# Two batches at a time in the body of a linear-attention and squared-ReLU kernel, ungated weight loads, and an order table in place of a planner

## The chip, the cores and the metric

One core of a Trainium2 chip runs the whole program. Its engines are TensorE (PE in the profile; PEld is its weight loads), VectorE (DVE), ScalarE (ACT), GpSimd (POOL) and SyncE (SP), beside 16 DMA engines that SP, ACT and POOL feed through queues of their own. The metric is device time in microseconds, from launch to end. A profiled execution also has a span: from the first to the last instruction that the profile shows.

## The reference

Four batches, eight heads, 768 steps, 48 channels per head. For each batch and head a 48 x 48 state is carried over the steps; its output goes, 384 channels wide, into a two-layer network with a squared ReLU.

```python
for t in range(S):
    kt, vt, rt = k[:, :, t], v[:, :, t], r[:, :, t]
    cur = einsum('bhd,bhe->bhde', u[None] * kt, vt)
    y[:, :, t] = einsum('bhd,bhde->bhe', rt, state + cur)
    state = w[None, :, :, None] * state + einsum('bhd,bhe->bhde', kt, vt)
x = y.transpose(0, 2, 1, 3).reshape(B * S, H * D)      # 3072 x 384
g = np.maximum(x @ w_in, 0.0) ** 2                      # w_in: 384 x 2048
return g @ w_out                                        # w_out: 2048 x 384
```

All inputs and the output are float32; the kernel multiplies in bfloat16.

## The kernel before

**Units.** The 768 steps are cut into 6 chunks of 128, so there are 24 units (chunk, batch), numbered 4 * chunk + batch. Within a chunk the recurrence becomes matrix products. Each unit goes through these steps, which the planner's keys and the order table name:

- `rt`, `kt`, `vt`: loads of r, k, v. For units 0 to 5 r and k come as two half loads with a row order of their own; later units load the 192-byte rows of all heads in one DMA. r and k are issued by SP, v by POOL, there behind a small copy (`gate`) that waits until k of the unit before has landed.
- `scale` (DVE, twice): r and k times powers of the decay, into `rkw` (bfloat16, heads padded to 64).
- `rkT`: r and k turned to channel-major. Units 0 to 5 by PE transposes (`turn`) and ACT copies, with `kb`, `kbT` turning k back; later units by one transposing DMA on SP (L476).
- `rk` (DVE), `at` (PE, L521: 8 products of 64 rows, k times q), `mask` (DVE, twice), `s` (PE: row sums `d` for the current step's term, and the state product), `dv`, `sadd`, `sdec` (DVE), `stb` (ACT), `y` (PE, L576 and, from chunk 1, L582), `yb` (DVE).
- `xT`: the unit's output turned, by PE and ACT (`xturn`) for units 0 to 5, later by a transposing DMA on SP (L600).
- `m1` (PE, L623): input product, 4 steps of 12 matmuls of 128 x 128 columns, each with its own 128 columns of `w_in_q` as stationary operand; `relu` (ACT), `sq` (ACT or DVE).
- `m2` (PE, L647): output product, 4 steps of 4 matmuls with 384 columns; `osb` (ACT) and `out` (SP store). The last unit does m2 in two halves (L663).

**Weights.** `w_in_q` and `w_out_q` are four tiles each, cast on the way by POOL's DMAs: `I.0` to `I.3` and `O.0` to `O.3`. Each waits behind a `gate` copy until some r or k has landed (`FRONT`, L277; L442).

**Order.** Nothing is scheduled at run time: each engine runs its instructions in the order in which the program emits them. Before, `Plan.run` (L47) makes this order on the host from costs, ranks and due times; `GROUPS` and `PAIRED` (L281, L282) leave every unit by itself. While PE has nothing to do in the first 16 planned microseconds, it runs `fill` matmuls (L380) on a constant tile. `bank` gives each product one of eight PSUM banks.

Of the kernel before, what the change touches and what calls it, by code (L numbers as in the profile page):

```python
# [16 lines left out]
class Plan:  # L17

    def __init__(self, lags, cold, spare, turns):
        self.turns = turns
        self.lags = lags
        self.cold = cold  # L30
        self.spare = spare
        self.steps = []
        self.at = {}
        self.users = {}
        self.place = {}

    def add(self, key, engine, cost, emit, needs=(), rank=0.0, new=(), uses=(), move=None):
        kind, which = (key[0], key[1] if len(key) == 2 else key[1:]) if isinstance(key, tuple) else ("", key)
        rank = self.turns.get(kind, {}).get(which, rank)
        s = dict(key=key, engine=engine, cost=cost, emit=emit, rank=rank, new=new, move=move)  # L40
        s["needs"] = [n for n in needs if n is not None]
        self.at[key] = s
        self.steps.append(s)
        for x in tuple(new) + tuple(uses):
            self.users.setdefault(x, []).append(s)

    def run(self, room, banks, count):  # L47
        todo = {}
        for s in self.steps:
            todo.setdefault(s["engine"], []).append(s)  # L50
        for mine in todo.values():
            mine.sort(key=lambda s: s["rank"])
        rings = {name: [] for name in room}
        free = {e: 0.0 for e in todo}
        queues = {e: [] for e in todo}
        held = {n: None for n in range(count)}
        since = {n: 0.0 for n in range(count)}
        begin, until, tight, loose = self.spare
        free["SP"] = 0.74
        held[0] = "fill"  # L60
        order = []
        t = 0.0
        left = len(self.steps)
        tiny = 1e-9

        moved, chained, left_pe, to_pe, near = self.lags

        def ready(s, e):
            if s["move"]:
                return s["end"] + moved + s["move"][4]  # L70
            if s["engine"] == "PE":
                return s["end"] + (chained if e == "PE" else left_pe)
            return s["end"] + (to_pe if e == "PE" else near)

        marks = []

        def mark(s):
            for e in ("PE", ""):
                heappush(marks, ready(s, e))

        def done(s, e):
            return "end" in s and ready(s, e) <= t + tiny

        def fits(s):
            e = s["engine"]
            names = [x[0] for x in s["new"]]
            for name in set(names):
                if name in banks:
                    continue
                ring, m = rings[name], room[name]  # L90
                for n in range(len(ring) - m, len(ring) - m + names.count(name)):
                    if n >= 0 and not all(done(x, e) for x in self.users[ring[n]]):
                        return False
            wanted = [name for name in names if name in banks]
            if wanted:
                for n, x in held.items():
                    if x not in (None, "fill") and all(done(u, e) for u in self.users[x]):
                        held[n], since[n] = None, max(u["end"] for u in self.users[x])
                if sum(x is None for x in held.values()) < len(wanted):
                    return False  # L100
                for name in set(wanted):
                    mine = sum(x is not None and x[0] == name for x in held.values())
                    if mine + wanted.count(name) > banks[name]:
                        return False
            return True

        while left:
            if held[0] == "fill" and t > until:
                held[0] = None
            for e, mine in todo.items():  # L110
                if free[e] > t + tiny:
                    continue
                if e == "PE" and t < begin - tiny:
                    free[e] = begin
                    continue
                for s in mine:
                    if s["move"] and sum(x[1] / x[0]["move"][0] * x[0]["move"][3] for x in queues[e]) > 1.5:
                        continue
                    if all(done(self.at[k], e) for k in s["needs"]) and fits(s):
                        mine.remove(s)  # L120
                        left -= 1
                        for x in s["new"]:
                            if x[0] in banks:
                                n = 4 + x[1] if x[0] == "log" else min((n for n in held if held[n] is None), key=lambda n: since[n])
                                held[n] = x
                                self.place[x] = n
                            else:
                                rings[x[0]].append(x)
                        s["start"] = t
                        free[e] = t + s["cost"] * (self.cold[1] if e == "PE" and t < self.cold[0] else 1.0)  # L130
                        if s["move"]:
                            queues[e].append([s, s["move"][0], free[e] + s["move"][2]])
                        else:
                            s["end"] = free[e]
                            mark(s)
                        order.append(s)
                        break
                else:
                    if e == "PE" and t < until:
                        free[e] = t + (tight * self.cold[1] if t < self.cold[0] else loose)  # L140
                        order.append(dict(key="fill", emit=self.fill, start=t, end=free[e], engine="PE"))
            heads = [q[0] for q in queues.values() if q]
            moving = [x for x in heads if x[2] <= t + tiny]
            whole = sum(x[0]["move"][1] for x in moving)
            later = [f for f in free.values() if f > t + tiny]
            while marks and marks[0] <= t + tiny:
                heappop(marks)
            later += marks[:1]
            later += [x[2] for x in heads if x[2] > t + tiny]
            later += [t + x[1] * whole / x[0]["move"][1] for x in moving]  # L150
            if not later:
                if left:
                    raise ValueError("nothing can go on: " + str([s["key"] for m in todo.values() for s in m[:3]]))
                break
            step = min(later) - t
            t += step
            for x in moving:
                x[1] -= step * x[0]["move"][1] / whole
                if x[1] <= 1e-7:
                    queues[x[0]["engine"]].pop(0)  # L160
                    x[0]["end"] = t
                    mark(x[0])
        return order
# [3 lines left out]
def kernel(  # L167
# [20 lines left out]
    NQ = 4  # L188
    NPE = 6
    NKE = 6  # L190
    NPY = 6
    NPAD = 8
    NVB = 8
    LATE = (0.2, 0.2, 0.4)
    MOST = 3
    SQUARES = 'AAAMAAAM'
    TURNS = {
        "": {
            "zeros": 38.551
        },  # L200
        "O": {
            0: 76.019, 1: 91.228, 2: 107.535, 3: 7
        },
        "rt": {
            0: -83.003, 1: -66.162, 12: 22.377, 13: 28.231, 14: 28.49, 15: 33.657, 3: -36.29, 5: 1.476, 8: 3.237
        },
        "kt": {
            0: -80.584, 1: -55.486, 10: 19.508, 11: 20.529, 2: -47.443, 6: 2.358
        },
        "at": {  # L210
            0: -3.958, 11: 34.671, 4: -16.745, 7: 10.944
        },
        "mask": {
            (1, 0): -39.238, (10, 0): 33.02, (2, 1): 25.375, (5, 1): 1.515
        },
        "sadd": {
            1: 9.124, 4: 45.244
        },
        "rk": {
            2: 13.012, 7: 14.32, 8: 68.867, 9: -12.042  # L220
        },
        "sums": {
            11: 49.353, 2: -24.778, 8: 5.082
        },
        "dv": {
            2: -26.848, 7: 34.164, 9: -12.993
        },
        "stb": {
            2: -9.741, 4: 57.421
        },  # L230
        "scale": {
# [294 lines left out]
    def at_pair(i):  # L526
        at(i)
        at(i + 1)
# [361 lines left out]
```

## Time and profile before

| | |
|---|---|
| median of 3 runs (lowest to highest) | 175.59 us (175.58 to 175.65) |
| the profiled execution's span | 174.3 us |
| PE, PEld busy | 166.7 us (96%), 134.7 us (77%) |
| ACT, DVE, POOL busy | 132.1, 121.1, 40.0 us |
| DMA packets | 76474, 28.93 MB |
| `fill` matmuls | 98 |

The profiled execution's own time is its span and what lies around it; the median of the runs is 1.3 us above the span. A row of the chain of waits gives start, duration and what was on the chain: an engine and source line with the number of instructions, or a DMA. In a table by stretches of time the columns are busy time of each engine with its number of instructions, the granted TensorE clock, the mean share of the 16 DMA engines and the rate. The page's busy times count overlaps once; "mean ns" is one instruction's own duration, which for pipelined matmuls is longer than their distance.

### The profile page before, as it was taken

To read this page: it belongs to the slowest core of one execution; us is meant where nothing else is said; L and a number is where in the kernel's file an instruction comes from. 1 tells how busy PE (TensorE), PEld (TensorE's weight loads), DVE (VectorE), ACT (ScalarE), POOL (GpSimd) and SP (SyncE) were. 2 spreads that over 40 slices of the span, in tenths; PEclk is the share of its full clock that TensorE was granted. 3 is DMA by queue.
4 is the path that set the end of the run, shared out by engine and by line. 5 is a ranking of instruction groups with operands and counts; after the bars stand their busy time and mean duration, and the time that the engine had idled before them with its cause. 6 is when DMAs were issued, how large, how long until landed. Compare 5 with 4: busy or idle time off the path is not lost.

```text
span 174.3 us, 5795 instructions
## 1 busy us (share of the span) xinstructions
PE 166.7 (96%) x2390; PEld 134.7 (77%) x2390; DVE 121.1 (70%) x252; ACT 132.1 (76%) x268; POOL 40.0 (23%) x84
## 2 busy tenths in 40 slices
PE   7978899999999999999999999999999999999991
PEld 6766799887687787886896787869787698877871
DVE  7869976615999899977986799794989635531010
ACT  3946999999458797886968876939994869948640
POOL 7866890300140220302032202203202000000000
PEclk9999999999999999999999999999999999999999
DMA  4889999999999999999999999999999971130121
GB/s 97 228 179 246 232 218 193 185 221 118 170 201 164 178 154 209 200 214 170 231 142 183 156 237 214 218 177 141 186 200 175 271 180 26 26 111 6 47 81 56
DMA packets 76474, 28.93 MB, mean 166 GB/s; under 512 B 65440, under 2 KB 75296, under 8 KB 76448
## 3 DMA queue, kind: packets, MB, share of 16 engines
q1 hardware_dynamic: 70848, 20.56, 69.8%
q0 software_dynamic: 5312, 7.87, 23.9%
q8 instruction: 18, 0.29, 0.8%
q10 hardware_dynamic: 288, 0.15, 0.4%
q14 instruction: 8, 0.07, 0.1%
HBM read 20.50 MB, written 4.72 MB: 145 GB/s over the span
## 4 chain that ended last, share of the span: by engine, by line
PE 81%; DMA 11%; SPq 4%; issue 1%; DVE 0%; POOL 0%; POOLq 0%
PE bank L623 35%; PE bank L647 33%; DMA w_in_q<-in_moe_w_in_dram 5%; SPq L436 4%; DMA rkT<-rkw 4%; PE bank L521 4%; DMA rt<-in_r_dram 2%; PE bank L576 2%; PE bank L582 2%; PE bank L546 2%; PE bank L663 2%; PE bank L541 1%; PE bank L487 0%; PE bank L607 0%; POOL gate L442 0%
## 5 line engine op out<-in xcount | busy, mean ns | idle before, releaser
L623 PE MATMUL bank<-xT,w_in_q 128*128 128x128 bf16 x1152 | 70.7, 219 | 0.1
L623 PEld LDWEIGHTS <-w_in_q 128*128 128x128 bf16 x1152 | 66.5, 98 | 3.1 <-DMA w_in_q<-in_moe_w_in_dram 0.3
L647 PE MATMUL bank<-w_out_q,g 128*128 128x384 bf16 x368 | 66.9, 326 | 0.0
L631 ACT ACTIVATE gr<-bank 128x512 f32<-128x512 f32 x96 | 54.3, 599 | 13.6 <-PE bank L623 13.3
L647 PEld LDWEIGHTS <-g 128*128 128x128 bf16 x368 | 33.3, 98 | 19.8
L638 ACT ACTIVATE g<-gr 128x512 bf16<-128x512 f32 x72 | 43.7, 637 | 0.4
L533 DVE TENSOR_TENSOR am<-bank,smask 128x512 bf16<-128x512 f32 x48 | 31.3, 682 | 3.3 <-PE bank L521 3.1
L640 DVE TENSOR_TENSOR g<-gr 128x512 bf16<-128x512 f32 x24 | 16.5, 686 | 21.5 <-ACT gr L631 21.5
L465 POOL COPY gate<-kt 128x1 f32<-128x1 f32 x22 | 5.8, 266 | 80.9 <-DMA kt<-in_k_dram 80.9
L654 ACT COPY osb<-bank 128x384 f32<-128x384 f32 x23 | 11.0, 483 | 15.8 <-PE bank L647 15.8
L467 POOL DMA_DIRECT2D vt<-in_v_dram x24 | 21.4, 893 | 5.9 <-issue 1.6
L555 DVE TENSOR_TENSOR dv<-vb,bank 128x384 f32<-128x384 bf16 x24 | 13.2, 548 | 5.3 <-PE bank L546 3.4
L513 DVE TENSOR_TENSOR rk<-rkT 128x512 bf16<-128x512 bf16 x24 | 10.0, 417 | 7.7 <-DMA rkT<-rkw 4.3
L591 DVE TENSOR_TENSOR yb<-bank,dv 128x384 bf16<-128x384 f32 x24 | 13.2, 550 | 2.8 <-PE bank L582 2.4
L471 ACT CAST vb<-vt 128x384 bf16<-128x384 f32 x24 | 12.4, 518 | 0.0
L458 DVE TENSOR_TENSOR rkw<-rt,wpos 128x384 bf16<-128x384 f32 x18 | 9.8, 550 | 1.4 <-DMA rt<-in_r_dram 1.4
L458 DVE TENSOR_TENSOR rkw<-kt,wneg 128x384 bf16<-128x384 f32 x18 | 9.9, 549 | 0.9 <-DMA kt<-in_k_dram 0.9
L567 ACT CAST stb<-st 128x384 bf16<-128x384 f32 x20 | 10.4, 519 | 0.0
L380 PE MATMUL bank<-warm 128*128 128x128 bf16 x98 | 9.3, 248 | 1.1 <-DVE warm L322 1.1
L521 PE MATMUL bank<-rkT 64*128 64x128 bf16 x192 | 9.5, 219 | 0.2
L494 ACT COPY rkT<-bank 128x512 bf16<-128x512 bf16 x12 | 6.8, 588 | 3.0 <-PE bank L487 3.0
L563 DVE TENSOR_TENSOR st<-st,wend 128x384 f32<-128x384 f32 x16 | 8.8, 549 | 0.0
(74 smaller groups left out, 129.1 us busy)
## 6 DMA issues: line engine op xcount, KB each, us to landing
vt<-in_v_dram POOLq DMA_DIRECT2D x24, 192.0 KB, 4.6
out_dram<-osb SPq DMA_DIRECT2D x23, 192.0 KB, 4.0
rt<-in_r_dram SPq DMA_DIRECT2D x18, 192.0 KB, 4.5
kt<-in_k_dram SPq DMA_DIRECT2D x18, 192.0 KB, 4.3
w_in_q<-in_moe_w_in_dram POOLq DMA_DIRECT2D x4, 384.0 KB, 7.9
w_out_q<-in_moe_w_out_dram POOLq DMA_DIRECT2D x4, 384.0 KB, 12.7
kt<-in_k_dram SPq DMA_DIRECT2D x12, 96.0 KB, 4.3
rt<-in_r_dram SPq DMA_DIRECT2D x11, 96.0 KB, 4.2
```

Source lines behind the costliest of these rows:

```text
L458: nc.vector.tensor_tensor(t["rkw"][:, x, :, :, :D], pair(src), pair(wneg if x else wpos), ALU.mult)
L467: nc.gpsimd.dma_start(out=tiles[i]["vt"], in_=v[b, :, c * C : (c + 1) * C, :].rearrange("h s d -> s h d"))
L471: nc.scalar.copy(tiles[i]["vb"], tiles[i]["vt"])
L521: nc.tensor.matmul(out=t["at"][o][:, p, :], lhsT=t["rkT"][sl, 1, p, :], rhs=t["rkT"][sl, 0, p, :], start=True, stop=True,)
L533: nc.vector.tensor_tensor(am, t["at"][o], smask.unsqueeze(1).to_broadcast([C, HP, C]), ALU.mult)
L555: nc.vector.tensor_tensor(t["dv"], t["vb"], t["d"].unsqueeze(2).to_broadcast([C, H, D]), ALU.mult)
L591: nc.vector.tensor_tensor(t["yb"], t["y"], t["dv"].rearrange("p h d -> p (h d)"), ALU.add)
L623: nc.tensor.matmul(out=t["h", s][:, a], lhsT=turned, rhs=chunks[c]["xT"][:, n, b : b + m, :], start=(n == 0), stop=(n == NK - 1),)
L631: nc.scalar.activation(t["gr", s], t["h", s], AF.Relu)
L638: nc.scalar.activation(g, x, AF.Square)
L640: nc.vector.tensor_tensor(g, x, x, ALU.mult)
L647: nc.tensor.matmul(out=t["o"], lhsT=chunks[units[i][0]]["g"][:, f, units[i][1], :], rhs=w_out_q[f // 4][:, f % 4, :], start=(f == 0), stop ...
```

## The change

From unit 6 on (`NH = 6`) the body works on pairs of units 2j, 2j+1 of one chunk. One DMA loads r of both, one k of both, one v of both, and v is now issued by SP (`vtS`), without gate. One transposing DMA turns both units' `rkw` (`rkD`), one both units' `yb` (`xD`). `rk`, `vb` and `at` run once for two units; `m1` of a pair has 8 steps of 6 matmuls with 256 columns. `scale`, `mask`, `s`, `dv`, `y`, `yb`, `m2` and the stores stay per unit, and `relu` and `sq` keep their number and shape.

```diff
-    loads = ctx.enter_context(tc.tile_pool(name="loads", bufs=7))
+    loads = ctx.enter_context(tc.tile_pool(name="loads", bufs=4))
...
+    def both(src, i):
+        c, b = units[i]
+        return src[b : b + 2, :, c * C : (c + 1) * C, :].rearrange("b h s d -> s (b h) d")
...
+            nc.sync.dma_start(out=whole.rearrange("s b h d -> s (b h) d"), in_=both({"rt": r, "kt": k}[name], i))
...
-    def weights(gated, q, which):
-        nc.gpsimd.tensor_copy(gate, tiles[gated[1]][gated[0]][:, H - 1, :1])
+    def weights(which, q):
...
-            src = moe_w_out.rearrange("(q a ki) d -> q ki a d", q=NQ, a=NF // NQ)
+            src = moe_w_out.rearrange("(q ki a) d -> q ki a d", q=NQ, a=NF // NQ)
...
     def load_v(i):
-        if i > 1:
-            nc.gpsimd.tensor_copy(gate, tiles[i - 1]["kt"][:, H - 1, :1])
+        if i >= NH:
+            nc.sync.dma_start(out=whole.rearrange("s b h d -> s (b h) d"), in_=both(v, i))
...
     def turn_dma(i):
-            out=t["rkT"].rearrange("p a h c -> p (a h) c"),
-            in_=t["rkw"].rearrange("p a h o e -> p (a h o e)"),
+            out=whole.rearrange("p u a h c -> p (u a h) c"),
+            in_=rkw_b[i // 2 % NPAD].rearrange("p u a h o e -> p (u a h o e)"),
...
     def at(i):
+        for j in range(i, i + (2 if i >= NH else 1)):
...
     def x_dma(i):
-        nc.sync.dma_start_transpose(out=x_tile(i), in_=tiles[i]["yb"])
+            out=chunks[c]["xT"][:, b : b + 2].rearrange("p b n c -> p (b n) c"),
+            in_=two("yb", i, work, [C, dm]).rearrange("p u d -> p (u d)"),
...
-                turned = w_in_q[f // 4][:, n, f % 4 * 128 : f % 4 * 128 + 128]
+                turned = w_in_q[f // 4][:, n, f % 4 :: 4]
                 nc.tensor.matmul(
-                    out=t["h", s][:, a], lhsT=turned, rhs=chunks[c]["xT"][:, n, b : b + m, :],
+                    out=t["h", s][:, a], lhsT=turned, rhs=chunks[c]["xT"][:, b : b + m, n, :],
```

`w_out_q` now holds four neighbouring rows of w_out in each partition, and the stationary operand of `m1` takes every fourth column of `w_in_q`, so that both products number the 2048 hidden channels alike. `xT` keeps a unit's three blocks together. The units 0 to 3 have a bank of their own for the sums `d`, so these are issued ahead of `s`. The buffers for loads hold 4 pairs (8 units) where there were 7 units.

`Plan`, its costs, ranks and due times are gone. A text, `ORDER`, lists all steps one after the other (`name.unit.step@bank`), and each engine runs its own in this order; `fill.n` stands for n fill matmuls, 104 in all. Its beginning, the stretch around the last pair's `at`, and its end:

```diff
+ORDER = """
+kt.0.0 kt.0.1 rt.0.0 rt.1.0 I.0 rt.1.1 ids fill.25 log@4567 ktA.1.0 lnat.0 rt.2.0 vt.0 lnat.1 w.0 fill.1 cols@1
+kt.1.1 w.1 upper copied kt.2.0 end scale.0.0 wk kt.2.1 vt.1 scale.0.1 wr fill.14 turn.0.0@2 rt.2.1 turn.0.1@3 zeros
+rkT.0.0 rt.3.0 vt.2 rkT.0.1 scale.1.0 rt.3.1 uwb fill.16 at.0@14 rk.0 kb.0@5 mask.0.1 turn.1.0@6 I.3 kbT.0 rt.4.0
+mask.0.0 fill.4 d.0@7 rkT.1.0 I.2 vb.0 vb.1 rt.4.1 dv.0 wend fill.17 s.0@2 y.0@3 scale.1.1 kt.3.0 vb.2 vt.3 yb.0
+kt.3.1 fill.13 turn.1.1@4 sadd.0 I.1 rkT.1.1 kt.4.0 fill.4 xturn.0@5 xT.0 rk.1 vt.4 kt.4.1 fill.8 kb.1@1 stb.0
+scale.2.0 at.1@67 kbT.1 kt.5.0 d.1@3 scale.2.1 m1.0.0@2 vt.5 mask.1.0 rt.5.0 s.1@4 turn.2.0@5 relu.0.0 mask.1.1 O.0
+turn.2.1@1 rkT.2.0 fill.2 m1.0.3@6 sadd.1 O.3 rt.5.1 sqA.0.0 dv.1 y.1@0 relu.0.3 scale.3.0 O.1 rt.6 yb.1 stb.1
+turn.3.0@2 rkT.2.1 scale.4.0 xturn.1@7 rkT.3.0 sqD.0.3 kt.5.1 kb.2@5 xT.1 at.2@43 rk.2 O.2 kbT.2 turn.4.0@6 mask.2.0
+m1.1.2@0 rkT.4.0 kt.6 scale.3.1 d.2@1 vb.3 s.2@2 m1.1.0@7 mask.2.1 relu.1.2 sadd.2 turn.3.1@5 sqA.1.2 m1.0.2@4 dv.2
...
+mask.19.1 m2.14.3 scale.23.1 s.20@4 s.19@6 osb.14 dv.20 at.20@5321 rkD.22 dv.19 y.19@0 mask.20.0 m1.16.0@7 mask.21.1
...
+sqA.16.6 at.22@7420 sqA.16.4 s.22@5 m1.18.4@6 mask.23.0 mask.23.1 m2.17.2 relu.18.4 dv.22 m1.18.6@2 sqA.18.4
...
+m2.23.0@4 osb.22 out.22 m2.23.1@5 osb.23.0 out.23.0 osb.23.1 out.23.1
+"""
```

More of the change, by code (lines that the diff above doesn't have):

```diff
@@ L14 @@
 PSUM = bass.MemoryType.PSUM
[L17 to L163, printed above, removed]
@@ new lines @@
+    steps = dict(
+        log=spread_log, lnat=log_at, w=power_four, wk=lambda: power(wneg, down), wr=lambda: power(wpos, up),
+        ids=identities, upper=upper, zeros=zeros, cols=spread_columns, copied=copy_columns, uwb=u_columns,
+        end=end_columns, wend=end_blocks, I=lambda q: weights("I", q), O=lambda q: weights("O", q),
+        rt=lambda *a: load("rt", *a), kt=lambda *a: load("kt", *a), ktA=lambda *a: load("kt", *a, nc.scalar), rtA=lambda *a: load("rt", *a, nc.scalar),
+        vt=load_v, vtS=load_v, vb=cast_v, scale=scale, turn=turn, rkT=lambda i, x=None: evict_rk(i, x), rkD=turn_dma, kb=turn_back, kbT=evict_back, d=lambda i: diag_sums(i, bank("d", i)[:, :H]),
+        rk=rk, at=at, mask=mask, s=sums, dv=diag_v, sadd=state_add, sdec=state_decay, stb=state_cast,
+        y=y_mm, yb=evict_y, xturn=x_turn, xT=evict_x, xD=x_dma,
+        m1=lambda i, s: mm1(i, size(i), s), relu=lambda i, s: relu(i, size(i), s),
+        sqA=lambda i, s: square(i, size(i), s, True), sqD=lambda i, s: square(i, size(i), s, False),
+        m2=lambda i, q: mm2(i, q) if i < NU - 1 else mm2_half(i, q),
+        osb=lambda i, n=None: evict_o(i) if n is None else evict_half(i, n),
+        out=lambda i, n=None: store(i) if n is None else store_half(i, n),
+    )
@@ L863 @@
+    for word in ORDER.split():
+        what, _, where = word.partition("@")
+        name, *a = what.split(".")
+        if name == "fill":
+            for _ in range(int(a[0])):
+                fill()
+            continue
+        a = [int(x) for x in a]
+        if where:
+            place.update(zip(names(name, *a), (int(x) for x in where)))
+        steps[name](*a)
 _INS = ['r', 'k', 'v', 'w', 'u', 'moe_w_in', 'moe_w_out']
```

492 lines of the change are left out of this document (163 added, 329 removed).

## The prediction

> **What bounds the kernel now.** I read the page first: busy times, the slices, the DMA queues, the costliest groups.
>
> ```profile
> PE 166.7 (96%) x2390; PEld 134.7 (77%) x2390; DVE 121.1 (70%) x252; ACT 132.1 (76%) x268; POOL 40.0 (23%) x84
> DMA  4889999999999999999999999999999971130121
> GB/s 97 228 179 246 232 218 193 185 221 118 170 201 164 178 154 209 200 214 170 231 142 183 156 237 214 218 177 141 186 200 175 271 180 26 26 111 6 47 81 56
> q1 hardware_dynamic: 70848, 20.56, 69.8%
> q0 software_dynamic: 5312, 7.87, 23.9%
> L623 PEld LDWEIGHTS <-w_in_q 128*128 128x128 bf16 x1152 | 66.5, 98 | 3.1 <-DMA w_in_q<-in_moe_w_in_dram 0.3
> L465 POOL COPY gate<-kt 128x1 f32<-128x1 f32 x22 | 5.8, 266 | 80.9 <-DMA kt<-in_k_dram 80.9
> w_in_q<-in_moe_w_in_dram POOLq DMA_DIRECT2D x4, 384.0 KB, 7.9
> ```
>
> PE is the bound, and the DMA engines are hardly less busy: nine tenths or more from the third slice to the 32nd. So the chain of waits comes next, in order of time.
>
> ```profile
> 13.73 8.19 DMA w_in_q<-in_moe_w_in_dram
> 21.96 2.18 PE bank L623 x36
> ...
> 41.46 0.22 PE bank L487 x4
> ...
> 43.85 0.22 PE bank L502 x4
> ...
> 45.16 0.08 PE bank L541 x4
> 45.24 0.19 PE bank L546 x4
> ...
> 48.03 0.20 PE bank L576 x8
> 48.23 0.17 PE bank L582 x4
> 48.40 0.33 PE bank L521 x8
> 48.73 0.76 PE bank L647 x4
> 49.49 0.17 PE bank L607 x3
> ...
> 49.93 0.65 PE bank L647 x4
> 50.58 0.67 PE bank L623 x12
> ...
> 130.27 6.50 DMA rkT<-rkw
> ...
> 149.42 0.33 PE bank L521 x8
> ...
> 168.08 2.65 PE bank L663 x32
> 170.76 0.29 DVE osb L675
> ```
>
> Up to 21.96 us the chain hangs on loads, the last of them the second quarter of w_in. From there to 170.76 us it is PE without a break worth naming, 148.8 us, but for one transposing DMA at 130 us. Then 3.5 us are left for the last eviction and store (174.3 - 170.8). So the time is a start, PE's remaining work, and a tail that the change leaves alone.
>
> **Remaining PE work, before.** The rows above price each step: m1 0.67, m2 0.65, `d` 0.08, state product 0.19, `y` 0.20 and 0.17, a turn or a turn back 0.22, `xturn` 0.17. `at` is 0.33, but the m2 step behind it takes 0.76 in place of 0.65, so 0.44 in all. At 21.96 us there remain by the program 94 m1 steps, 92 m2 steps and the last 2.65, 20 `at`, 20 `d`, 16 state products, 21 and 20 of the two parts of `y`, 5 turns of either kind, 3 `xturn`: 63.0 + 62.5 + 8.8 + 1.6 + 3.0 + 7.6 + 1.1 + 0.5 = 148.1. The chain says 148.8; 0.7 us are small losses.
>
> **The pairs on PE.** An m1 pair step has 6 matmuls with 256 columns. The row of L663 holds 16 with 256 and 16 with 128 columns: (2.65 - 16 x 0.67 / 12) / 16 = 0.110 each, so 0.66 a step, and 8 steps are 5.27 where two units took 8 x 0.67 = 5.36. A pair of `at` runs 16 matmuls in a row. This is what the stream itself costs, by the weight loads' timeline:
>
> ```profile
> 48.33 0.22 PEld L521 LDWEIGHTS <-rkT 64*128 64x128 bf16 x8
> ```
>
> Eight stream in 0.22 of the 0.44; the other 0.22 is getting in and out, and a pair pays it once. Nine pairs save 9 x 0.09 + 9 x 0.22 = 2.8 us. The floor is 0 for `at` (if nothing overlaps), the ceiling some 0.3 more by the 384-column row. Relu and squares keep number and shape, `rk` and `vb` save a few start-ups on engines with slack (ACT 76%, DVE 70%): nothing on PE's path.
>
> **Where the dense part starts.** In the new order PE is dense from `m1.1.2`, for which the third weight tile issued by POOL (`I.2`) and unit 1's output must be there. After it remain 22 single m1 steps and 72 pair steps, the 62.5 of m2, 3 single and 9 pair `at`, 22 `d`, 18 state products, 22 and 20 parts of `y`, 7 turns, 4 `xturn`: 14.7 + 47.5 + 62.5 + 7.3 + 1.8 + 3.4 + 7.8 + 1.5 + 0.7 = 147.1. When does it start? The rows of the front now (POOL's and PE's timeline, then stretches of time):
>
> ```profile
> 10.38 0.74 POOL L445 DMA_DIRECT2D w_in_q<-in_moe_w_in_dram  x1 [0.27 <-issue]
> ...
> 17.13 0.78 POOL L445 DMA_DIRECT2D w_in_q<-in_moe_w_in_dram  x1 [0.27 <-issue]
> 18.56 0.76 POOL L445 DMA_DIRECT2D w_in_q<-in_moe_w_in_dram  x1 [0.27 <-issue]
> ```
>
> ```profile
> 17.56 0.83 PE L623 MATMUL bank<-xT,w_in_q 128*128 128x128 bf16 x12
> ```
>
> ```profile
> 0.00:15.00 15.00, 11.96 (x170) 10.16 (x171) 11.00 (x38) 8.82 (x19) 11.52 (x31) 1.00 0.77 174
> 15.00:140.00 125.00, 123.97 (x1816) 99.47 (x1815) 100.54 (x198) 101.55 (x207) 28.49 (x54) 1.00 1.17 193
> 140.00:175.00 35.00, 30.72 (x409) 25.04 (x407) 9.59 (x17) 21.70 (x44) 0.00 (x0) 1.00 0.21 63
> ```
>
> The gates held w_in's quarters to 10.4, 13.7, 17.1 and 18.6 us. Without them `I.0` goes out with POOL's first DMAs, `I.3` and `I.2` right behind `uwb`. The bytes ahead of `I.2`'s end are three quarters (3 x 384 KB), three v (3 x 192 KB) and some 20 half loads of r and k (96 KB): 3.7 MB. At 174 GB/s, 2.6 MB are through at 15 us; the rest at 193 to the page's best slices, some 250, takes 4.4 to 5.7 us: about 20 us, or earlier by up to 1 us if the first DMAs start fuller. I take 19.2. The other condition is unit 1's output: now both first units are through at 17.56, and the new order asks no more of DVE by then. `I.1` is needed 3.6 us of PE work later, with 0.6 MB more to load (3 us): no further wait. The bounds of the start are 16.5 (half of the loads' congestion gone) and 25.0 (the third quarter as late as now: 17.1 + 7.9). The 104 fills only stand where PE waits anyway; so did the 98.
>
> **The body.** Loads, POOL and SP. POOL's 80.9 us behind gates cost nothing and come off nothing. On SP, a pair's load replaces two, so v's nine issues come beside 18 fewer for r and k and 18 fewer transposes; a pair load lands later, but by the table it is issued well ahead (`rkD.22` goes out 9 us of PE work before `at.22`). What SP's queue gains is v itself: 18 units x 0.197 MB = 3.5 MB move from q0, where 23.9% of the span (41.7 us) moved 7.87 MB, 5.3 us per MB, to q1 with 69.8% (121.7 us) for 20.56 MB, 5.9 per MB: 2.2 us more of DMA time, in the same 16 engines that are full already. More weighs when it is wanted. The last `at` has 21 us of PE work behind it now (149.42 to 170.76); in the new table `at.22` has 24 m1 pair steps, 25 m2 steps, the last 2.65 and 1 us of sums, 35.6 us. So the transfers must be done at about 168 - 36 = 132 us, not 140. All queues hold 95% of 174.3 us, 165.6; 7.4 of it (0.21 x 35) lies after 140 now, and as much will lie behind. That leaves 160 with v, of which the first 15 us may take 15, so 145 in 115 us (130 with 2 us to land): a share of 1.26, where 15 to 140 us now has 1.17. If 1.17 is a ceiling the data come 9 us late; if SP's own waits made it, nothing is late. DVE is near its limit too (100.5 of 125 us) and gets the same work in less time. I take 1.2 us of PE waiting, near the lower end, because the share counts packets that wait for each other and PE lost next to nothing at 1.17.
>
> The Trainium skill, DMA: Bandwidth & Descriptors (Specifications), says that pieces under 512 B miss the line rate, which speaks against v as 192-byte rows on SP. The two queues' rows agree, 5.9 against 5.3 us per MB; the rule gives no larger price here.
>
> **Sum.** 19.2 + 147.1 + 0.7 + 1.2 = 168.2, with the tail 3.5 a span of 171.7, and with the 1.3 us by which the median of the runs (175.59) lies above the profiled span (174.3), 173.0 us.
>
> **The rivals.**
>
> The DMA engines become the bound (slower). Price: half of the 9 us, less what I took already: 173.0 - 1.2 + 4.5 = 176.3 us, up to 180.8 with all of it. It decides the sign from 3.8 us of waiting on (175.6 - 171.8). For it: the DMA row of nines, and the DMA wait at 130 us that already is on the chain. Against it: the order can hold four pairs of loads ahead.
>
> The loads crowd each other in the front (slower): with the weights among the first r and k, `I.2` lands no earlier than the third quarter does now, 25.0 us. Then 173.0 + 5.8 = 178.8 us. Against it: fewer bytes are ahead of it than there were.
>
> Strided weights load slowly (slower). Today's loads are contiguous, and `d` shows how fast they can be: 4 matmuls, each with 128 columns of its own to load, in 0.08 us. Taking every fourth column might lose that. The dearest row is 98 ns each, with nothing overlapped: the 288 matmuls of units 0 to 5 would take 98 for 56 ns, 12.1 us, so 185 us; the pairs' 110 ns hide it. The Trainium skill, SBUF — State Buffer (Door 1), says lines of 16 bytes want at least two hits each; every fourth bfloat16 still has two. By that rule the term is nothing; no run here shows it.
>
> The gain does not come: the dense part starts no earlier than 21.9 us (second quarter as now) and the pairs' 2.8 us go into waits: 175.6, no change.
>
> Better: the start is set by unit 1's output alone, 16.7 us, and nothing waits in the body: 173.0 - 2.5 - 1.2 = 169.3 us.
>
> **How the numbers follow.** Forecast, 171 to 174.8 us: 0.52. Better: 0.13. DMA bound: 0.22. Crowded front: 0.05. Strided weights: 0.03. No change: 0.05. About 0.2% is what a measurement of this kernel can tell from no change. Faster is the first two and the mild edge of the third, 0.67; same 0.05; slower 0.28. The range leaves out the far end of the better case, the worst of the DMA case and the strided weights: 169.3 to 178.5; the likeliest case's own range is 171 to 174.8.
>
> **What would show it.** `at` of a pair should take 0.66 us with its way out, an m1 pair step 0.66. On the chain, PE should be unbroken from 18 to 20 us on; a start beyond 22.7 us would undo the gain, and its releaser would be a DMA of w_in. DMA rows for `rkT`, `xT` or v between PE's in the chain from 40 to 132 us, by more than 1 us in sum, would show the DMA case, and DVE rows there that DVE's work has been packed too tightly. L623's distance in units 0 to 5 above 56 ns would show strided weights. I am wrong if these sums do not fit: start + 147.1 + waits + 3.5.

## The result, and the profile after

| | before | after |
|---|---|---|
| median of the runs (lowest to highest, number) | 175.59 us (175.14 to 177.21, 14) | 174.44 us (173.39 to 175.87, 14) |
| ratio, 95% interval | | 0.993, 0.9905 to 0.9956 |
| profiled execution's span | 174.3 us | 172.2 us |
| that execution's own time | not listed | 173.95 us |

The change makes the kernel 1.15 us faster; 2.6 us were forecast (173.0 us). The changed kernel was run twice more later, beside the kernel before: 174.85 us (0.9917, 0.9882 to 0.9951) and 175.24 us (0.9961, 0.992 to 1.0002). The median of its 37 runs is 174.56 us. They lie between 173.0 and 177.5 us, a wide scatter that matters below. A ratio leaves out the runs that took over 1.5% longer than the fastest of their kernel, so it can differ from the quotient of two medians.

The page after, the rows that answer to those of before, with the weight loads of the input product:

```profile
PE 165.0 (96%) x1964; PEld 135.8 (79%) x1964; DVE 121.9 (71%) x243; ACT 131.4 (76%) x255; POOL 15.9 (9%) x36
DMA  3999999999999999999999999999192013011031
q1 hardware_dynamic: 88416, 23.99, 69.0%
q0 software_dynamic: 2624, 4.33, 12.4%
L493 PEld LDWEIGHTS <-w_in_q 128*128 128x128 bf16 x720 | 64.0, 113 | 3.3
```

The row of nines in the slices of DMA time now ends at the 28th slice, 120 us, where it ended at the 32nd, 139 us. All queues hold 82.7% of 172.2 us (with 1.3% of the small ones), 142.4 us, where they held 165.6: **DMA time fell by 23 us** although v's bytes moved to q1. That queue now takes 118.8 us for 23.99 MB, 5.0 us per MB; it took 5.9.

The chain of waits after (start, duration, what was on it):

```profile
3.64 6.47 DMA rt<-in_r_dram
...
10.21 0.57 DVE rkw L303
...
14.81 1.02 DVE rkw L303 x2
15.84 1.20 DVE am L377 x2
17.04 0.47 DVE st L424
17.50 0.46 DVE dv L420
...
18.34 0.56 DVE yb L456
...
77.60 0.66 PE bank L493 x6
78.25 0.55 PE bank L369 x16
78.81 0.76 PE bank L517 x4
...
81.08 7.86 DMA rkT<-rkw
...
88.98 0.62 PE bank L369 x16
...
166.10 2.65 PE bank L533 x32
```

PE's timeline at the two places that matter (in brackets the idle time before a row, and what ended it):

```profile
18.49 0.40 PE L333 MATMUL bank<-identb,rkw 128*128 128x128 bf16 x4 [0.78 <-DVE rkw L303]
...
20.07 0.83 PE L493 MATMUL bank<-xT,w_in_q 128*128 128x128 bf16 x12
...
88.98 0.62 PE L369 MATMUL bank<-rkT 64*128 64x128 bf16 x16 [0.94 <-DMA rkT<-rkw]
```

Read along the sum: the dense part starts with `m1.1.2` at 20.07 us (forecast 19.2). From there to the end of the last product, 168.75, are 148.7 us. If PE's work is the forecast's 147.1 us, 1.6 us of losses fill the rest; 0.7 + 1.2 were forecast as losses. The tail is 172.2 - 168.75 = 3.45 (3.5). So the profiled span is 0.5 us above the forecast of 171.7.

The losses by stretches of time, before and then after (busy time of PE, PEld, DVE, ACT, POOL, then clock, DMA share, GB/s):

```profile
25.00:60.00 35.00, 35.00 (x483) 27.70 (x481) 25.10 (x49) 28.61 (x60) 6.80 (x12) 1.00 1.11 180
60.00:90.00 30.00, 30.00 (x471) 24.73 (x469) 26.76 (x55) 24.72 (x50) 5.84 (x10) 1.00 1.18 190
90.00:115.00 25.00, 25.00 (x354) 19.51 (x352) 19.70 (x39) 19.80 (x41) 4.34 (x8) 1.00 1.22 196
115.00:140.00 25.00, 24.76 (x349) 19.50 (x348) 19.38 (x38) 18.71 (x38) 3.56 (x6) 1.00 1.20 196
```

```profile
25.00:60.00 35.00, 35.00 (x507) 27.83 (x505) 31.63 (x61) 27.20 (x55) 0.00 (x0) 1.00 1.14 217
60.00:90.00 30.00, 28.89 (x334) 24.40 (x333) 26.22 (x50) 27.96 (x55) 0.00 (x0) 1.00 1.14 207
90.00:115.00 25.00, 25.00 (x251) 19.68 (x249) 20.57 (x41) 17.42 (x34) 0.00 (x0) 1.00 1.09 209
115.00:140.00 25.00, 25.00 (x319) 21.03 (x318) 21.50 (x40) 19.24 (x38) 0.00 (x0) 1.00 0.43 103
```

PE idles 1.11 us from 25 to 140 us, before 0.24. After 115 us the DMA engines move 103 GB/s at a share of 0.43, before 196 at 1.20. SyncE's queue fits that: the last k load (unit 23 before, pair 22 after) goes out 14 us sooner. The first row is of before, the others of after:

```profile
129.63 0.53 SPq L438 DMA_DIRECT2D kt<-in_k_dram  x1
```

```profile
75.21 0.57 SPq L278 DMA_DIRECT2D kt<-in_k_dram  x1
75.88 1.11 SPq L553 DMA_DIRECT2D out_dram<-osb  x1
...
79.11 1.85 SPq L278 DMA_DIRECT2D kt<-in_k_dram  x2
81.08 4.76 SPq L322 DMA_TRANSPOSE rkT<-rkw  x1
...
115.45 0.45 SPq L278 DMA_DIRECT2D kt<-in_k_dram  x1
```

The transpose that PE waits for at 88.98 is issued at 81.08, behind stores and loads that are wanted much later, and takes 4.76 us to issue.

### The profile page after: what moved, and what is told of

Its sections match the earlier page's. It is cut to its first block, busy times and chain, and to the rows that moved or that the text cites. A ratio compares the mean times of both kernels' runs of the same rounds, so it can differ in the third digit from the quotient of the medians.

```text
span 172.2 us, 4759 instructions
## 1 busy us (share of the span) xinstructions
PE 165.0 (96%) x1964; PEld 135.8 (79%) x1964; DVE 121.9 (71%) x243; ACT 131.4 (76%) x255; POOL 15.9 (9%) x36
## 3 DMA queue, kind: packets, MB, share of 16 engines
q1 hardware_dynamic: 88416, 23.99, 69.0%
q0 software_dynamic: 2624, 4.33, 12.4%
## 4 chain that ended last, share of the span: by engine, by line
PE 81%; DMA 8%; DVE 4%; ACT 2%; SPq 2%; issue 1%; DVEq 0%
PE bank L517 34%; PE bank L493 31%; DMA rkT<-rkw 5%; DMA rt<-in_r_dram 4%; PE bank L369 3%; PE bank L441 2%; PE bank L398 2%; PE bank L447 2%; SPq L281 2%; PE bank L533 2%; PE bank L410 1%; PE bank L333 1%; PE bank L216 1%; DVE rkw L303 1%; DVE am L377 1%
## 5 line engine op out<-in xcount | busy, mean ns | idle before, releaser
L493 PE MATMUL bank<-xT,w_in_q 128*128 128x256 bf16 (+1 forms) x720 | 72.1, 251 | 0.0
L493 PEld LDWEIGHTS <-w_in_q 128*128 128x128 bf16 x720 | 64.0, 113 | 3.3
L508 ACT ACTIVATE g<-gr 128x512 bf16<-128x512 f32 x68 | 42.0, 640 | 0.8
L510 DVE TENSOR_TENSOR g<-gr 128x512 bf16<-128x512 f32 x28 | 19.3, 688 | 24.1 <-ACT gr L501 23.9
L316 ACT CAST vb<-vt 128x768 bf16<-128x768 f32 x9 | 7.6, 841 | 3.4 <-DMA vt<-in_v_dram 3.4
L216 PEld LDWEIGHTS <-warm 128*128 128x128 bf16 x104 | 8.7, 124 | 1.2 <-DVE warm L161 1.0
L369 PE MATMUL bank<-rkT 64*128 64x128 bf16 x192 | 8.0, 219 | 0.9 <-DMA rkT<-rkw 0.9
L424 DVE TENSOR_TENSOR st<-bank,st 128x384 f32<-128x384 f32 x16 | 8.6, 550 | 0.2 <-PE bank L398 0.2
L441 PE MATMUL bank<-vb,am 128*128 128x48 bf16 x192 | 8.7, 183 | 0.0
L357 DVE TENSOR_TENSOR rk<-rkT 128x1024 bf16<-128x1024 bf16 x9 | 6.2, 686 | 3.4 <-DMA rkT<-rkw 3.4
```

The costliest lines, as they stand in the source:

```text
L216: nc.tensor.matmul(out=banks[0][:, :128], lhsT=warm, rhs=warm, start=True, stop=True)
L369: nc.tensor.matmul(out=t["at"][o][:, p, :], lhsT=t["rkT"][sl, 1, p, :], rhs=t["rkT"][sl, 0, p, :], start=True, stop=True,)
L441: nc.tensor.matmul(out=y[:, 2 * p + o, :], lhsT=t[f"am{o}"][:, p, :], rhs=t["vb"][:, 2 * p + o, :], start=(o == 0 and p == 0), stop=c == 0 ...
L493: nc.tensor.matmul(out=t["h", s][:, a], lhsT=turned, rhs=chunks[c]["xT"][:, b : b + m, n, :], start=(n == 0), stop=(n == NK - 1),)
L508: nc.scalar.activation(g, x, AF.Square)
L510: nc.vector.tensor_tensor(g, x, x, ALU.mult)
```

## The experiments

"Changed kernel" below is the kernel after. Medians have their lowest and highest in brackets; ratios are against the kernel before, run beside them (175.5 to 176.0 us).

### The front: four tries at the 0.9 us

Unit 1's r lands at 10.1 us, behind `I.0` that is now issued early. Is that all?

```diff
-kt.0.0 kt.0.1 rt.0.0 rt.1.0 I.0 rt.1.1 ...
+kt.0.0 kt.0.1 rt.0.0 rt.1.0 rt.1.1 ...
-... kt.2.1 vt.1 scale.0.1 ...
+... kt.2.1 vt.1 I.0 scale.0.1 ...
```

> The changed kernel with one word of the order table moved: the first quarter of w_in (I.0) is issued behind the second v load instead of ahead of everything. Theory A (the ungated I.0 takes the DMA engines from the first r and k, so that DVE waits 3.8 us for unit 1's r and the dense part starts at 20.1 us): r of unit 1 lands before 7.5 us instead of 10.1, DVE's 3.8 us wait falls under 1 us, the dense part starts 1 to 2.5 us earlier, and the time falls by 0.8 to 2 us against the changed kernel's 174.4, to 172.4 to 173.6. Rival B (the start is set by the bytes that all must land before I.2 and I.1, whatever their order): I.2 lands no earlier than its 19.1 us, the start stays at 20 us within 0.5 us and the time at 174.4 within 0.4.

178.65 us (174.75 to 180.14). Both theories missed. The profiled run is one of the slowest, 179.86 us. In it r came in time, but the third v, now behind `I.0`, landed at 14.1 us and held ScalarE and so PE. PE's timeline of this run:

```profile
15.20 0.61 PE L345 MATMUL bank<-identb,rkT 128*128 128x128 bf16 x4 [2.83 <-ACT rkT L337]
...
16.40 1.45 PE L493 MATMUL bank<-xT,w_in_q 128*128 128x128 bf16 x12
```

The last row shows more: twelve matmuls take 1.45 us, not 0.83. TensorE's granted clock has fallen to 0.50 and stays there to about 21 us; the runs of this edit at full clock took 174.75 to 179.11 us, so the clock is only a part of the loss.

Further behind, after the third v (`rt.3.1 uwb I.0 fill.16`):

> The first quarter of the input weights goes behind the first three v loads on GpSimd's queue (the experiment before had put it ahead of the third one, which then came at 14.1 us and held ScalarE). Theory A (the quarter's early issue is what makes unit 1's r late, 10.1 us against 6.3 before): the r lands by 7 us, the third v by 10 us, the quarter by 15.5 us; the dense products start at 18.6 to 19.2 us instead of 20.1, and the time is 173.3 us, 1.1 below the control. Theory B (the front is bound by its bytes, and putting one load behind makes another late): start at 20 us or later, 174.4 us or more.

176.14 us (174.37 to 180.19), ratio 0.9983 (0.9946 to 1.0019). v and r are early now, and the quarter itself is late; PE's waits of this run:

```profile
PE bank L493 <- DMA w_in_q<-in_moe_w_in_dram: 3.4, 2, 2.4
```

The first place again, with ScalarE's `vb.2` moved from ahead of `rkT.1.1` to behind `relu.0.0`:

> The first experiment again (first quarter of the input weights behind the second v load), and with it ScalarE's cast of unit 2's v moved behind the turned r and k of unit 1 and the first relu: in the first experiment that cast waited until 14.1 us and held ScalarE for 3.7 us. Theory A (the front is a matter of which wait stands in which queue): ScalarE copies unit 1's turned k by 11.5 us, the first input product starts by 14.2 us (15.3 in the changed kernel), the dense products at 18.6 to 19.2 us, and the time is 173.4 us, 1.2 below the 174.6 of the changed kernel. Theory B (the front is bound by its bytes): the first input product still starts at 15 us or later, and the time is 174.5 us or more.

175.77 us (173.69 to 177.05), 0.996 (0.992 to 1.0). The first input product starts at 14.61 us, 0.7 sooner, but the second waits 0.7 us for a later quarter, `yb` and the turned k come 0.4 us late each, and the dense part starts at 20.2 us as ever. The clock weighs in here too: in seven of the twelve runs its mean is 0.98 to 0.99 (175.69 to 177.05 us), in the other five it is full (173.69 to 174.69 us, median 174.03). Of the 37 runs of the changed kernel six have such a clock.

Last, fewer bytes with the order kept:

```diff
     def load_v(i):
...
+        if 2 <= i < NH:
+            tiles[i]["vt"] = tiles[i % 2]["vt"]
+            return
```

> The changed kernel without the v loads of units 2 to 5 (those units use the v of units 0 and 1 again): 0.79 of some 4.4 MB that come in the first 21 us, on the queue of GpSimd behind the first quarter of the input weights. Theory A (the start is set by unit 1's r, late behind that quarter, and the vector engine's chain after it): the r still lands at about 10 us, the last wait of the front ends within 0.5 us of the control's, and the time is within 0.4 us of the control, 174.2 to 174.8 us. Theory B (the front is bound by all its bytes): the later quarters land 2 us sooner, the last wait ends 1 us or more sooner, and the time is 173.5 us or less.

174.05 us (173.63 to 177.18), 0.9893 (0.9845 to 0.9942): between the two forecasts, so the trace has to tell. The vector engine's timeline shows r as late as ever:

```profile
10.24 0.62 DVE L303 TENSOR_TENSOR rkw<-rt,wfour 128x384 bf16<-128x384 f32 x1 [3.79 <-DMA rt<-in_r_dram]
```

PE's wait for the vector engine in the front ends at 18.6 us, the control's at 18.5, and there is one more of 0.5 us that ends at 22.5. The third weight tile landed at 18.5 us, a microsecond sooner than the control's, and the dense part still starts at 20.2. What this run gains it gains in the body, where no wait for a transpose is left. So the start is set by unit 1's r behind `I.0` and the chain of DVE work after it, as theory A says, but none of three orders of the same loads lowered the median: wherever `I.0` goes, it, a later quarter, a v or the r comes late.

### The pairs' price on PE

Input product in single columns again (two matmuls of 128 columns for one of 256), then the second unit's `at` one PE step later:

```diff
-                    out=t["h", s][:, a], lhsT=turned, rhs=chunks[c]["xT"][:, b : b + m, n, :],
+                    out=t["h", s][:, a, x], lhsT=turned, rhs=chunks[c]["xT"][:, b + x, n, :],
...
```

> The changed kernel with each 256-column matmul of the input product done as two of 128 columns (864 instead of 432 matmuls in the body, with as many weight loads). If PE's work is what sets the time, by the distances of 109 and 56 ns between matmuls the span grows by 432 x 3 ns = 1.3 us, and the time by 1.0 to 1.5 us. If something else (DMA, DVE) paces the body, by less than 0.5.

```diff
-        for j in range(i, i + (2 if i >= NH else 1)):
+        for j in range(i + second, i + second + 1):
...
```

> The changed kernel with the two units' at no longer back to back: the second unit's 8 matmuls come one step of PE later, so that another product lies between. If getting into and out of the 64-row product costs 0.2 us each time, 9 x 0.2 = 1.8 us more PE time, and 1.5 to 2.2 us more in the whole. If the gain of the pairs were only the matmul count, nothing.

180.08 us (177.73 to 181.84), ratio 1.0158 (1.0095 to 1.022), and 176.95 us (175.01 to 179.53), 1.003 (0.9991 to 1.0068). By the distances between all matmuls, waits left out, PE's work rises by 1.3 and by 1.9 us. The rest, about 4 us in the first, is new stalls of 1 to 2 us in places that the edit does not touch, and in its profiled run (181.84 us, the slowest of six) a dense part that starts 1.6 us later behind a fall of the clock. Together the two pairs are worth 3.2 us of PE work; 2.8 were forecast (0.8 for m1, 2.0 for `at`).

### v's queue

```diff
-            nc.sync.dma_start(out=whole.rearrange("s b h d -> s (b h) d"), in_=both(v, i))
+            nc.gpsimd.dma_start(out=whole.rearrange("s b h d -> s (b h) d"), in_=both(v, i))
```

> The changed kernel with v of the body issued by POOL's queue again, still two units at once and without gate. Theory A (v between the transposes on SP's queue makes them late: the 1.0 us that PE waited for the transposing DMA at 87.8 us): PE's waits behind 40 us fall from 1.5 us to under 0.5, time 0.6 to 1.2 us lower than 174.4. Rival B (that wait is a collision of the transposing DMA with an instruction fetch at 84.2 us and has nothing to do with v): waits of 0.3 to 2 us stay somewhere in the body, at another place, and the time is within 0.5 us of 174.4.

184.95 us (182.61 to 185.95), ratio 1.0491 (1.0435 to 1.0547): both theories fell. With nothing ahead of it, GpSimd's queue sends four pair loads of v out between 20.3 and 31 us, a half load of k issued at 19.6 us takes 22.1 us to land (14.5 in the changed kernel), and PE waits 3.7 us at 38.8. This run's stretches:

```profile
39.00:42.00 3.00, 0.00 (x0) 0.00 (x0) 0.57 (x2) 0.42 (x1) 0.00 (x0) 0.91 0.89 171
42.00:45.00 3.00, 2.49 (x19) 2.14 (x20) 3.00 (x7) 1.15 (x2) 0.00 (x0) 0.50 1.05 210
45.00:48.00 3.00, 3.00 (x29) 2.28 (x27) 0.44 (x3) 1.64 (x4) 0.00 (x0) 0.50 1.20 251
48.00:51.00 3.00, 3.00 (x50) 2.62 (x50) 2.35 (x5) 2.02 (x4) 0.00 (x0) 0.96 0.97 191
```

The column before the DMA share is the granted clock: 0.50 for some 6 us after the wait, so by an estimate from these rows (6 us at half pace lose 3) a wait of 3.7 us costs nearly twice that. On SyncE's queue v is held back by what stands ahead of it, and that is worth having here.

### The body: place in the queue, or bytes

First the control, the changed kernel beside the next three:

> The changed kernel as it stands, beside the next three on one chip. If the four edits before this were slow through themselves, it gives 174.4 us again (173.9 to 174.9) with body losses (matmul time beyond the nominal distances, from 25 us on) of 1.2 to 2.0 us, and the wait for the turned r and k of unit 14 (the q k^T products of unit 14 near 88 us) of 0.7 to 1.3 us among them. If the chip or the day made them slow, it gives 175.5 or more.

174.85 us (173.01 to 176.56): the four edits before it were slow through themselves. Its wait at unit 14 is there again. Then three ways to take it away. By order:

```diff
-... scale.15.0 m1.8.7@1 scale.15.1 sqA.8.0 out.7 ... kt.18 ... kt.20 ... sqA.8.6 rkD.14 s.12@6
+... scale.15.0 m1.8.7@1 scale.15.1 rkD.14 sqA.8.0 out.7 ... kt.18 ... kt.20 ... sqA.8.6 s.12@6
```

> The transpose of unit pair 14 is issued on SyncE's queue ahead of an output store and the k loads of 18 and 20 instead of behind them. Theory A (place in the queue: its input was written by 75.5 us, but it was issued at 81.08): it is issued by about 79 us, the wait of 0.9 us before the q k^T of unit 14 goes, no other comes, and the time is 173.4 us, 1.0 below the control. Theory B (the transfers are at capacity, so a transposing transfer that goes ahead makes another late): the wait shows up at another unit, and the time stays within 0.3 us of the control. Theory C (any edit of the fixed order costs 1 us or more of new stalls elsewhere): 175 us or more.

175.93 us (172.68 to 176.85); the ratio, 0.9894 (0.9812 to 0.9976), rests on two of its six runs. The waits of PE in the profiled one, the slowest (176.85 us):

```profile
PE bank L333 <- DVE rkw L303: 3.0, 2, 2.2
...
PE bank L493 <- DVE st L424: 0.9, 1, 0.9
PE bank L441 <- ACT gr L501: 0.7, 1, 0.7
PE bank L517 <- ACT g L508: 0.6, 1, 0.6
```

The wait for `rkT` is gone, and waits of 0.9, 0.7 and 0.6 us at other places have taken over. The worse front (3.0 us) goes with a granted clock of 0.51 from 11 to 14 us, which a later transpose cannot cause. One run reached 172.68 us, so what this order is worth without that is not settled.

By bytes, v of all later pairs left out:

```diff
     def load_v(i):
...
+        if i >= NH + 2:
+            twos["vt", i // 2] = twos["vt", NH // 2]
+            return
```

> v is loaded for the pair 6, 7 alone in the body; the later pairs use that tile again, which leaves 8 of the 9 body loads of v out (3.1 MB, at 5 us of sixteen queues' time per MB some 1.0 us of 15 us each). Theory B (body stalls come from transfers near capacity): stalls from 25 us on fall from about 1.5 us to under 0.4, the time to 173.2 us or less, and it scatters by less than the control. Theory A (place in the queue): the wait for the transpose of unit 14 stays at 0.5 us or more, since the k loads and the store ahead of it are all still there; 174.0 us.

172.53 us (171.91 to 173.72), ratio 0.9818 (0.9776 to 0.986). Bytes and issues went together here; the next keeps the issues and their places, and loads two of sixteen heads:

```diff
...
+        n = 16 if i < NH + 2 else 2
...
-            nc.sync.dma_start(out=whole.rearrange("s b h d -> s (b h) d"), in_=both(v, i))
+            nc.sync.dma_start(out=whole.rearrange("s b h d -> s (b h) d")[:, :n], in_=both(v, i)[:, :n])
```

> The body's v loads from pair 8, 9 on stay where they are in SyncE's queue and take an eighth of the bytes (two of sixteen heads; the other heads are those of an earlier unit). Theory B1 (it is the bytes: eight loads of 2,048 packets of 192 bytes, some 15 us of DMA time): as with eight of nine loads left out, 172.5 us and no stall over 0.45 us from 25 us on. Theory B2 (it is the place of the loads in SyncE's queue, where each issue takes 0.4 to 1.6 us and everything behind it waits): stalls of 1 us or more from 75 us on as in the control, 174.4 us or more.

172.37 us (172.03 to 173.99), ratio 0.9832 (0.9777 to 0.9887). Its stretches, and the sum of PE's busy time in them:

```profile
60.00:90.00 30.00, 29.80 (x347) 25.05 (x345) 27.35 (x52) 27.87 (x56) 0.00 (x0) 1.00 0.94 189
90.00:115.00 25.00, 25.00 (x256) 20.03 (x254) 20.77 (x41) 18.75 (x37) 0.00 (x0) 1.00 0.82 169
115.00:140.00 25.00, 25.00 (x313) 20.60 (x310) 20.27 (x37) 18.73 (x37) 0.00 (x0) 1.00 0.29 70
sum 115.00, PE 114.80 PEld 93.50 DVE 100.23 ACT 92.57 POOL 0.00; mean PE 28.70 PEld 23.38 DVE 25.06 ACT 23.14 POOL 0.00
```

PE idles 0.20 us, as before the change, and the six runs scatter over 2 us where the 37 of the changed kernel scatter over 4.5. It is the bytes (and their packets, which go with them), not the places in the queue. This run also shows PE's work almost bare: its dense part takes 147.55 us, 19.86 to 167.41. A half dose (8 of 16 heads, `else 8`):

> The changed kernel with the v loads of the body's later eight pairs cut to half their heads: 7.7 us of DMA time taken away where the eighth took 13.4. If every us of transfer in the body costs alike, 174.6 less 7.7/13.4 of 2.3, 173.3 us. If there is a threshold, above which transposes come late and below which nothing is felt: 172.5 us as with the eighth, or 174.3 as with all.

173.29 us (172.33 to 174.34), ratio 0.9839 (0.979 to 0.9888): the median lies where the straight line had it. That does not rule a threshold out. The profiled run (173.57 us) waits in the body no longer than the one with the eighth, 0.20 us by the sum of the same stretches, and its dense part takes 147.50 us. It is slower by its front, where the clock falls:

```profile
11.00:14.00 3.00, 3.00 (x38) 3.00 (x35) 2.29 (x5) 1.82 (x4) 2.96 (x5) 0.50 1.16 252
...
sum 115.00, PE 114.80 PEld 94.02 DVE 100.21 ACT 92.49 POOL 0.00; mean PE 28.70 PEld 23.50 DVE 25.05 ACT 23.12 POOL 0.00
```

Three of these six runs have a mean clock below 0.99, two of the six with the eighth. The others took 172.33 to 173.35 us with half of v, 172.03 to 172.39 with the eighth: too few to tell a line from a step. And the eighth in the kernel before:

```diff
...
+        n = 8 if i < 8 else 1
-        nc.gpsimd.dma_start(out=tiles[i]["vt"], in_=v[b, :, c * C : (c + 1) * C, :].rearrange("h s d -> s h d"))
+        nc.gpsimd.dma_start(out=tiles[i]["vt"][:, :n], in_=v[b, :n, c * C : (c + 1) * C, :].rearrange("h s d -> s h d"))
```

> The kernel before, with the v loads of units 8 to 23 cut to one of eight heads (the other heads are an earlier unit's), the same cut that took the changed kernel from 174.6 to 172.4 us. Theory B1 (the change's order asks for the body's loads sooner, its last k load is issued at 115.5 us where the kernel before issued it at 129.6, so that only the changed kernel stalls on DMA): the kernel before had 0.4 us of stalls from 25 us on and has no more to give, 175.4 us, within 0.3 of it. Theory B3 (DMA load costs both kernels alike): 174 us or less.

175.42 us (174.81 to 176.36) beside 176.02, ratio 0.9979 (0.9951 to 1.0007): little or nothing. So only the changed kernel pays for DMA load.

Can order mend it after all? A second control, then three moves with all bytes kept, then two of the three:

```diff
-rkD.12 ... sadd.11 kt.16 sdec.10 ... yb.10 out.6 ... yb.11 m1.8.0@2 scale.14.0 osb.7 xD.10 scale.14.1 ... scale.15.1 ... out.7 ... rkD.14
+rkD.12 ... sadd.11 sdec.10 ... yb.10 ... yb.11 xD.10 m1.8.0@2 scale.14.0 osb.7 kt.16 scale.14.1 ... scale.15.1 rkD.14 out.6 ... out.7
...
-rt.22 ... vtS.22
+rt.22 vtS.22
```

> The changed kernel again, beside the run above on one chip: 174.4 to 174.9 us, with a wait for the turned r and k of unit 14 near 88 us of 0.7 to 1.3 us.

> The changed kernel with SyncE's queue in another order at three places: the transpose of pair 10's y stands ahead of the k load of 16 and an output store, the transpose of pair 14's r and k ahead of two stores and the k loads of 18 and 20, and the v load of 22 some 6 us sooner. Theory A (the body's stalls are places in a queue, to be mended by order with the same bytes): no stall over 0.45 us from 25 us on, the scatter as small as with the cut v (2 us), the time 172.9 us. Theory B (transfers near capacity: order only hands the wait on): stalls of 0.9 us or more in sum elsewhere, and 174.3 to 175.5 us, no better than the control at 174.4 to 175.2.

> The same without the move of pair 14's transpose: by theory A the wait of about 1 us for the turned r and k of unit 14 stays and the time is 173.8 us; by theory B 174.3 to 175.5 us as above.

175.24 us (173.74 to 177.54) for the control, 175.88 us (174.03 to 178.78) and 176.1 us (173.96 to 176.78) for the moves, ratios 0.9972 (0.9934 to 1.001) and 1.0035 (1.0014 to 1.0056). PE's timeline of the three moves:

```profile
110.35 0.62 PE L369 MATMUL bank<-rkT 64*128 64x128 bf16 x16 [1.34 <-DMA rkT<-rkw]
```

The wait of unit 14 is gone, and a later pair waits 1.34 us for the same kind of transpose. In these profiles order hands the wait on. No version that does all the work and beats the changed kernel was found.

## Why the prediction was right or wrong

**The direction and the main gain** were right. PE's remaining work is within 0.2 us of the sum (whose terms add up to 147.2, not 147.1): in the run with an eighth of v the dense part takes 147.55 us, of which PE waits 0.2 by the stretches above. A pair's `at` takes 0.55 + 0.11 on the m2 step behind it, the forecast 0.66, and a pair's m1 step 0.66. Unrolled, the pairs are worth 3.2 us, above the 2.8 (m1 was priced 0.5 too low).

**The size was wrong**, by 1.44 us, in three places:

1. *The step from the span to the runs: 0.95 us.* The forecast added the 1.3 us "by which the median of the runs lies above the profiled span". Each of the 37 runs of the changed kernel lies 1.74 to 1.85 us above its own span, and 108 runs of the kernel before 1.73 to 1.86. So the profiled execution of before took some 176.1 us, half a microsecond more than the median run, and its span stands as far above a median run's 173.8. That makes 0.48 us. The rest is that the profiled execution after, 173.95 us, lies 0.49 below its own median: stalls and start vary from run to run.
2. *The start: 0.87 us.* "The new order asks no more of DVE by then" failed. The third weight tile came when forecast (it landed at 19.1 us), but DVE took up unit 1's r at 10.2 us behind the ungated `I.0`, 3.9 us later than before (the row below is of before), and worked through the rest without a break from 14.8 to 18.9 us.

```profile
6.35 0.56 DVE L460 TENSOR_TENSOR rkw<-rt,wfour 128x384 bf16<-128x384 f32 x1 [0.39 <-DMA rt<-in_r_dram]
```

3. *The losses: forecast 1.9 us, 1.6 in the profile, some 2.1 in a median run if the 0.49 us above are put to them.* The size was right, the working was not. The DMA-bound case rested on a needed share of 1.26; DMA time fell by 23 us in place of the 2.2 us rise, the share was 1.09 to 1.14, and PE waited all the same. The share did not tell: before, 1.18 to 1.22 stood beside hardly a wait.

**The rivals.** A mild form of the DMA case is what happened: 2.2 us of the runs' median hang on v's bytes. Why after and not before? The rows show the last k load 14 us sooner, 207 to 217 GB/s from 25 to 115 us in place of 180 to 196, and a transpose queued behind loads for later; the runs show that bytes matter, and that none of the orders tried lowered the median. That the pace of the new order is the cause fits all of it but is argued: an order of the same steps at a slower pace was not built. A second rival, an instruction fetch in the middle of the transpose, is looked at in the last section. Strided weights cost no time: twelve matmuls of a single unit take 0.83 us as they did before (L493 after, L623 before). The loads themselves did become longer, 113 ns in place of 98, but stay hidden behind the matmuls. The crowded front showed itself in r, not in `I.2`, at 0.9 us instead of 5.8.

## What to carry to other kernels

Work saved on the busiest engine is worth what the transfers leave of it: look at when the last load must go out, not at the share of busy DMA time, and take away bytes as a test before rearranging a queue. Do not bridge from one profiled span to a median by their difference; compare each run with its own span first. Where an order is fixed by hand, price an edit with the stalls that it moves: of the six edits here that only moved entries of the order, none had a lower median than the order it started from. Look at the granted clock of each run as well, since an edit can make its falls more frequent: the five runs at full clock of one of the six have a median of 174.03 us, the 31 such runs of the changed kernel 174.4.

## What was not expected of the hardware

After a wait of 2.8 us (12.4 to 15.2 us in the first experiment) and after one of 3.7 us (v on GpSimd's queue) TensorE's granted clock was at half for about 6 us. Shorter waits sufficed in the front: in five profiled runs of edits that leave the front as it is (v on GpSimd's queue, single columns, the earlier transpose, one load of v, half of v) PE waits 1.8 to 2.4 us for unit 1's r, the clock is at half for the next 3.4 us, and the dense part starts at 21.2 to 21.7 us instead of some 20. A wait of 2.4 us in the second try of the front had no fall behind it. A fall in the front is worth some 1.5 us: with an eighth of v the four runs with a mean clock of 0.998 or more took 172.03 to 172.39 us, the two with 0.988 and 0.989 took 173.66 and 173.99. The Trainium skill, TensorE: Matmul & The Clock Gate (Part 1: The HAM clock gate), names windows of some 3.4 us both for falling to half and for coming back. The traces agree on the half, and the time at half was 3.4 us or, in the first two cases, 6.8 us; but a wait of 1.8 us was enough for a fall.

The transpose that PE waited for at 88.98 us stood still from about 84.9 to 86.1 us. These views of the DMA engines, 3 us in 40 slices each, are of the kernel after (from 83.5 us), of the first control (from 84) and of the run with an eighth of v (from 83). Each holds an instruction fetch of 16 KB, whose row is shown for the first:

```profile
DMA  9999999999999999999000000000000000089999
q8 instruction: 1, 0.02, 2.5%
...
DMA  9999999999999999990000000010000000109999
...
DMA  9999999999630074000003322599999999999999
```

The fetches begin at 84.2, 85.0 and 84.1 us. The second control shows the same as the first (fetch at 84.3, still from 85.0 to 86.3 us). In the profile after, three more transposes of r and k stand still for 1.2 to 1.3 us, at 43.8, 74.2 and 111.1 us, each half a microsecond behind such a fetch; two fetches, at 53.0 and 62.7 us, fell into the last 2 us or so of a transpose without a stop of that length. With all of v the standstill takes 1.2 to 1.4 us, longer than PE's wait of 0.9 to 1.0 us behind it; with an eighth of v the engines are empty for only some 0.4 us at a stretch. So PE might not have waited at unit 14 without the fetch, and fewer bytes may help by making this standstill short. Whether the fetch stops the transfer or only falls there each time was not tried.
